# New first loads, fillers ahead of the first products, a fourth buffer for transposed q and k, and a re-planned instruction list

## The chip, the cores and the metric

The kernel runs on one NeuronCore of a Trainium2 chip. The core has five instruction streams that run side by side, each strictly in its own order: TensorE (PE, matrix products), VectorE (DVE), ScalarE (ACT), GpSimd (POOL) and SyncE (SP, which issues DMAs). They wait for one another through semaphores. The metric is the device time of one execution in microseconds; lower is better. Beside the times stands the profile of one execution, whose span runs from the first to the last instruction.

## The reference

Two layers are computed: a linear attention with a feature map of exponentials, and then a layer normalization with a two-matrix feed-forward block and a residual.

```python
batch, n_heads, seq, head_dim = (8, 8, 576, 64);  d_feat = 128

def phi(x):
    proj = np.einsum('bhsd,df->bhsf', x, w_phi)
    proj = proj - np.max(np.abs(proj), axis=-1, keepdims=True)
    return np.concatenate([np.exp(proj), np.exp(-proj)], axis=-1)
q_p, k_p = (phi(q), phi(k))
kv = np.einsum('bhsf,bhsd->bhfd', k_p, v)
z = np.sum(k_p, axis=2)
num = np.einsum('bhsf,bhfd->bhsd', q_p, kv)
den = np.einsum('bhsf,bhf->bhs', q_p, z)[..., None] + 1e-06
x = (num / den)                      # heads side by side: (8, 576, 512)

mu = np.mean(x, axis=-1, keepdims=True)
var = np.mean((x - mu) ** 2, axis=-1, keepdims=True)
xn = (x - mu) / np.sqrt(var + 1e-06) * g_ln
out = x + np.maximum(xn @ w_ch1, 0.0) @ w_ch2      # 512 -> 2048 -> 512
```

Inputs and output are float32.

## The kernel before, in words

**Tiling.** The 8 batches are taken in 4 pairs. A pair has 8 units, each of two (batch, head) combinations, so there are 32 units, numbered n = 0 to 31. A unit's 2 x 576 positions are 8 full tiles of 128 ("main") and one tile with the last 64 of each half ("tails"). When a pair's units are done, its 1152 rows of x are normalized and go through the feed-forward block in 3 rounds of 384 rows: 16 groups of 4 first products (`hT_ps`, L1055) with a relu each (L1063 on DVE or L1065 on ACT), and then, for each of the 3 tiles of 128 rows, 16 second products (`ch_ps`, L1122), a scaling and residual, and a store from SP.

**A unit.** Its k and q are loaded as float32 (L347), brought to bf16 and transposed so that head_dim lies on the partitions. The first 8 units do that on PE with the identity (`a_trans`, L470 and L478) and copy from PSUM. From unit 8 (`QK_DMA`) on, `a_trans_dma` casts q and k into a bf16 buffer `b` (L536 on DVE, L538 on ACT, L540 on POOL) and SP issues a DMA transpose from it into `qkT` (L559). PE multiplies with w_phi (`pm` L622 and L628, `px` L580 and L581 for the tails, `pt` L637 in transposed form); DVE takes the maximum of absolute values (`m`, L686, L584); ACT takes the exponentials (`eb`, `ea`, `em`, `en`); POOL scales v by them (`vv`, L712 to L721); PE forms kv (L778, L783), which is copied (`KV`, L791), and the numerators (`num`, L829, L835); DVE multiplies and adds them (`numc`, L853, L859) and takes the inverse of the denominator (L863); POOL writes x (L869). Of x come the statistics (L982, L996), the centred rows `xc` (L1000) and their transposes `xT`: by PE for pair 0 (L946, L956), by a DMA transpose issued from SP after that (L969). The first weight matrix is scaled by g_ln in place on DVE after pair 0 (L450).

**Buffers.** There are 3 buffers of transposed q and k (`QB`), 2 of the cast ones (`b16_bufs`), 3 of loaded q, k and v. In PSUM there are two large tiles (A), three single banks (B) and one bank N.

**The order of the work.** The program is written first as a list of operations with the keys that they read and write. `Order.run` then plays it: each engine, when free, takes the ready operation of lowest rank; the order in which the operations were started is the order in which the instructions are emitted, and this holds for all five engines. A rank is a "latest start" counted back from the users plus an offset from the table `OFF` by kind of operation and stage (the first 4 units, the next 4, the rest); products of the feed-forward block also have due times (`DUE`, `BLOCK`). Where an operation names several engines, the one that takes it first has it. DMAs are played as an issue on the queue's engine followed by pieces on two modelled resources (hardware and software queues), and the data counts as there `LAND` us later. On the chip nothing of this planner is left but the order: an instruction that waits holds up all behind it on its engine.

**The start.** Ahead of the list a few instructions are emitted by hand: two loads of w_phi on ACT (L248, L249), the identity on POOL (masks.py), POOL's loads of the tails of q (L262), constants and zero fills on DVE, and two casts of w_phi to `wbk` on POOL (L272). In the list, operations without an instruction stand for their times. Until the planned time `WARM` (45 us), PE gets a filler (L1320), a product of a zero tile `wz` into a part of bank N that nobody reads, whenever it has nothing ready. One such product (L1317) opens the kernel.

Of the kernel before, what the change touches and what calls it, by code (L numbers as in the profile page):

```python
# [10 lines left out]
FP32 = mybir.dt.float32  # L11
# [6 lines left out]
def bcast(ap: bass.AP, dim: int, n: int) -> bass.AP:  # L18
# [5 lines left out]
DUE = 30.89  # L24
BLOCK = 115.16
RELU = -983.1
WARM = 45.0
X_DMA, QK_DMA = 1, 8
TILED = 4
LAND, TURN = 1.7, 0.013  # L30
# [3 lines left out]
        "load": 291.2, "trans": 30.0, "trans.copy": 30.0, "mixed": 49.3, "mixed.max": 23.2,  # L34
        "mixed.exp": 41.8, "k": 19.6, "k.max": 21.4, "k.em": -15.4, "k.exp": -46.8, "en": 15.6,
        "vv": -27.5, "q": 30.1, "q.max": 47.4, "q.em": 15.6, "tails": -42.2, "tails.exp": 7.3,
        "kv": -52.7, "kv.copy": 4.2, "num0": 51.4, "num1": -54.2, "num.dve": 32.4, "g1": 0.0,
        "g2": 0.0, "g3": 0.0, "put": -53.0, "ln": 201.7, "w1": -144.2, "w2": 207.3,
    },
    {  # L40
        "load": -11.5, "trans": -36.9, "trans.copy": 204.6, "mixed": 25.2, "mixed.max": -80.9,
        "mixed.exp": 132.7, "k": -79.5, "k.max": 146.3, "k.em": 53.6, "k.exp": -36.9,
# [6 lines left out]
        "load": 22.6, "trans": 17.7, "trans.copy": 96.2, "mixed": -96.6, "mixed.max": -70.2,  # L49
        "mixed.exp": -34.7, "k": -33.5, "k.max": -145.4, "k.em": -34.3, "k.exp": -84.1,  # L50
# [8 lines left out]
class Op:  # L59
    __slots__ = (  # L60
        "engines", "engine", "us", "emit", "rank", "lag", "deps", "users", "acquire", "release",
        "ready", "left", "number", "due",
# [9 lines left out]

class Order:


    def __init__(self, room):
        self.ops, self.wrote, self.read, self.room = [], {}, {}, dict(room)
        self.filler = (None, 0.0, 0.0, None)
# [28 lines left out]
    def run(self):  # L107
# [21 lines left out]
        while events:  # L129
# [10 lines left out]
            for engine, queue in waiting.items():  # L140
# [29 lines left out]
                elif isinstance(us, Op):  # L170
                    us = 1.1 if us.engine == "ACT" else 0.0
# [1186 lines left out]
```

## Time and profile before

| what | value |
|---|---|
| three runs | 382.18, 382.95, 384.82 us; median 382.95 |
| the profiled execution | 381.13 us, of which its span is 379.3 |
| busy, share of the span | PE 95%, ACT 68%, DVE 67%, POOL 54% |
| granted TensorE clock | 1.00 |
| DMA | 53.31 MB in 91133 packets, mean 141 GB/s |
| DMA transposes | 24 of q and k, 9 of x |

The three runs spread over 0.7% of their median. In the profile an engine is busy while an instruction of its own runs; issuing a DMA does not count, and shows under the engine's name with a q (SPq). A wait is put down to whatever released it last. "x24 | 6.5, 272 | 2.1" after an operation means 24 instructions, 6.5 us busy, 272 ns each, and 2.1 us of idle time of that engine just before them. PE's matmuls overlap, and their ends are modelled, so that the distance from start to start says more of its pace than the duration of one. In the table of stretches the columns are the stretch and its length, busy time and number of instructions of PE, its weight loads, DVE, ACT and POOL, the granted clock, and the DMA engines' share and rate.

### The profile page before, as it was taken

What the parts mean: (1) busy time and instruction counts of PE and PEld (TensorE: products, weight loads), DVE (VectorE), ACT (ScalarE), POOL (GpSimd) and SP (SyncE); (2) the same over time, 40 slices, a digit from 0 to 9 for tenths busy, and PEclk for the clock granted to TensorE, in tenths of its full rate; (3) what the DMA queues carried; (4) which work ended last, traced back from release to release, by engine and by line L of the source; (5) the groups of instructions that cost most, each with busy time, mean ns of one, the idle gap of its engine ahead of it and who ended that gap; (6) DMA issues with size and microseconds to landing.
All of it is one profiled execution on the core that took longest, in us unless ns stands there. A gap on an engine that the chain in (4) does not pass through costs nothing.

```text
span 379.3 us, 9487 instructions
## 1 busy us (share of the span) xinstructions
PE 358.9 (95%) x3626; PEld 220.2 (58%) x3626; DVE 254.8 (67%) x557; ACT 257.9 (68%) x574; POOL 204.4 (54%) x350
## 2 busy tenths in 40 slices
PE   4999979988999999999999999999999999999995
PEld 2988856554656555556566555556565555555543
DVE  3698998988999999987787999787749000000001
ACT  3877898968787876896877878786746534444420
POOL 4787878847785768463967835572562101111031
PEclk9999999999999999999999999999999999999999
DMA  8999699999975499956664274430104230101012
GB/s 223 274 223 279 182 225 214 200 276 248 259 203 181 84 229 178 238 108 202 151 167 128 65 158 139 90 61 7 51 13 89 76 88 29 28 30 54 30 55 84
DMA packets 91133, 53.31 MB, mean 141 GB/s; under 512 B 57488, under 2 KB 86544, under 8 KB 91088
## 3 DMA queue, kind: packets, MB, share of 16 engines
q1 hardware_dynamic: 86000, 47.66, 50.5%
q0 software_dynamic: 4384, 4.46, 7.6%
q10 hardware_dynamic: 704, 0.59, 0.6%
q8 instruction: 28, 0.46, 0.5%
q14 instruction: 17, 0.14, 0.1%
HBM read 36.77 MB, written 9.44 MB: 122 GB/s over the span
## 4 chain that ended last, share of the span: by engine, by line
PE 62%; DVE 18%; DMA 8%; issue 5%; POOL 2%; ACT 2%; SPq 1%; DVEq 0%; POOLq 0%; ACTq 0%
PE hT_ps L1055 25%; PE ch_ps L1122 24%; DVE m L686 5%; DMA qkT<-b 5%; DMA qx<-in_k_dram 3%; PE n_bank L783 2%; DVE st L982 2%; PE pm L628 2%; DVE numc L853 2%; DVE numc L859 2%; PE num L829 2%; DMA xT<-xc 1%; DVE hT L1063 1%; PE pt L637 1%; ACT eb L700 1%
## 5 line engine op out<-in xcount | busy, mean ns | idle before, releaser
L1055 PE MATMUL hT_ps<-xT,w 128*128 128x384 bf16 x768 | 152.1, 326 | 1.9 <-DMA xT<-xc 0.8
L1122 PE MATMUL ch_ps<-w,hT 128*128 128x512 bf16 x560 | 150.2, 379 | 0.1
L1055 PEld LDWEIGHTS <-w 128*128 128x128 bf16 x768 | 71.8, 98 | 59.2 <-issue 4.0
L1065 ACT ACTIVATE hT<-hT_ps 128x384 bf16<-128x384 f32 x120 | 59.1, 492 | 56.9 <-PE hT_ps L1055 56.3
L686 DVE TENSOR_REDUCE m<-pm 128x8 f32<-128x1024 f32 x64 | 76.8, 1212 | 13.9 <-PE pm L628 9.7
L869 POOL TENSOR_TENSOR x<-numc,rden 128x384 bf16<-128x384 f32 (+3 forms) x88 | 45.9, 537 | 55.4 <-DVE rden L863 53.6
L1122 PEld LDWEIGHTS <-hT 128*128 128x128 bf16 x560 | 50.8, 98 | 41.4 <-issue 1.6
L700 ACT ACTIVATE eb<-pm 128x1024 bf16<-128x1024 f32 x64 | 65.1, 1038 | 6.3 <-DVE m L686 6.3
L754 ACT ACTIVATE ea<-pt 128x1024 bf16<-128x1024 f32 x64 | 63.6, 1029 | 5.9 <-PE pt L637 5.5
L1141 POOL TENSOR_TENSOR o<-o,x 128x512 f32<-128x512 f32 x20 | 23.1, 1155 | 75.4 <-ACT o L1135 75.4
L1130 DVE SCALAR_TENSOR_TENSOR o<-ch_ps,rstd,x 128x512 f32<-128x512 f32 x15 | 11.1, 741 | 56.7 <-PE ch_ps L1122 56.6
L712 POOL TENSOR_TENSOR vv<-v,em 128x512 bf16<-128x512 f32 x32 | 34.0, 1062 | 20.3 <-issue 15.9
L1063 DVE TENSOR_SCALAR hT<-hT_ps 128x384 bf16<-128x384 f32 x72 | 39.0, 547 | 8.1 <-PE hT_ps L1055 7.7
L712 POOL TENSOR_TENSOR vv<-v,en 128x512 bf16<-128x512 f32 x32 | 34.0, 1062 | 0.0
L829 PEld LDWEIGHTS <-ea 128*128 128x128 bf16 x512 | 23.6, 97 | 9.9 <-issue 3.1
L783 PE MATMUL n_bank<-vv,eb 128*128 128x65 bf16 x512 | 26.9, 194 | 0.0
L540 POOL TENSOR_TENSOR b<-qk,one 128x1024 bf16<-128x1024 f32 x11 | 20.8, 1895 | 10.4 <-DMA qkT<-b 7.2
L783 PEld LDWEIGHTS <-eb 128*128 128x128 bf16 x512 | 22.3, 98 | 3.7 <-issue 0.3
L982 DVE BATCH_NORM_STATS2 st<-x 128x6 f32<-128x512 bf16 (+1 forms) x44 | 24.4, 580 | 0.0
L853 DVE TENSOR_TENSOR numc<-num,em 128x390 f32<-128x390 f32 (+1 forms) x40 | 20.4, 517 | 5.6 <-PE num L829 3.9
L1320 PE MATMUL n_bank<-wz 128*128 128x120 bf16 x333 | 23.0, 221 | 1.2 <-DVE KV L791 0.8
L829 PE MATMUL num<-KV,ea 128*128 128x65 bf16 x416 | 19.7, 193 | 2.0 <-ACT xT L958 0.9
(91 smaller groups left out, 460.3 us busy)
## 6 DMA issues: line engine op xcount, KB each, us to landing
qk<-in_k_dram SPq DMA_DIRECT2D x32, 256.0 KB, 4.3
v<-in_v_dram SPq DMA_DIRECT2D x32, 256.0 KB, 5.6
out_dram<-o SPq DMA_DIRECT2D x31, 256.0 KB, 2.4
qk<-in_q_dram SPq DMA_DIRECT2D x30, 256.0 KB, 5.8
w<-in_moe_w_ch_dram POOLq DMA_DIRECT2D x8, 512.0 KB, 11.1
out_dram<-o SPq DMA_DIRECT2D x10, 128.0 KB, 2.4
qx<-in_k_dram SPq DMA_DIRECT2D x16, 64.0 KB, 4.8
qx<-in_q_dram SPq DMA_DIRECT2D x14, 64.0 KB, 3.5
```

Of the source, the lines that this page charges most:

```text
L686: nc.vector.reduce_max(out=m, in_=ps, axis=AX.X, apply_absolute_value=True)
L700: nc.scalar.activation(eb, ps, AF.Exp, scale=(1.0, -1.0)[t])
L712: nc.gpsimd.tensor_tensor(out=u["vv"][:, t, 0:MX, 0:D], in0=vb[:, hh, :].rearrange("p (c d) -> p c d", d=D), in1=bcast(e[:, 0:MX], 2, D), ...
L754: nc.scalar.activation(u["EA"][:, t, 0:1024], u["pt"], AF.Exp, scale=(1.0, -1.0)[t])
L783: nc.tensor.matmul(ps[:, t, c // 4, :], EB[:, t, c, :], vv[:, t, c, :], start=False, stop=(t == 0 and c == MX - 1), skip_group_check=True,)
L829: nc.tensor.matmul(ps[t][:, i, :], ea(u, t, c), KV[:, t, c // 4, :], start=True, stop=True,)
L869: nc.gpsimd.tensor_tensor(out=dst, in0=st["numc"][ps_, i : i + n, 0:D], in1=bcast(st["rden"][ps_, i : i + n], 2, D), op=ALU.mult,)
L982: nc.vector.bn_stats(out=pr["st"][:, t, half or 0, :], in_=x[:, t, h0 * D : h1 * D])
L1055: nc.tensor.matmul(st["ps"], w1_sb[:, kc, jj * P : (jj + 1) * P], xT_bufs[(pair * NR + r) % XB][:, kc::KC, :], start=(kc == 0), stop=(kc = ...
L1063: nc.vector.tensor_relu(h_sb, st["ps"])
L1065: nc.scalar.activation(h_sb, st["ps"], AF.Relu)
L1122: nc.tensor.matmul(ch[t], hT[r, jj][:, rt * P : (rt + 1) * P], w2_sb[:, jj, :], start=(jj == 0), stop=(jj == JC - 1),)
```

## The change

The first loads are issued in another order and from other queues: w_phi half from SP and half from ACT, k of unit 0, its tails, k and q of unit 1 from SP, q and v of unit 0 from ACT, the tails of v from POOL. The casts of w_phi move from POOL to DVE, and the zero tile, wanted by the fillers, is written first. PE gets 28 fillers ahead of the list. There are 4 buffers of transposed q and k instead of 3, 3 of the cast ones instead of 2, and a cast is called for three units ahead instead of two. The planner's picture changes: loads, transposes and weights have landing times of their own; a transpose holds its queue for the transfers ahead of it (`Turn`); packets of two queues share only while both move; PE is 1.9 times slower until 5.6 us; and from unit 6 on, lags between engines, landings and packets are taken longer (`SLACK`). The offsets, `DUE` and `BLOCK` have other values, so the emitted order differs on all engines.

```diff
-DUE = 30.89
-BLOCK = 115.16
+DUE = -6.82
+BLOCK = 144.95
+COLD, FIRST = 5.6, 28
+SLACK = ((0.2, 0.0, 0.0, 1.0), (0.35, 1.2, 2.0, 1.05))
-X_DMA, QK_DMA = 1, 8
-LAND, TURN = 1.7, 0.013
+X_DMA, QK_DMA, AHEAD = 1, 8, 3
+LAND, LAND_T, LAND_W, TURN, BARRIER = 2.0, 1.1, 2.6, 0.013, 0.4
...
-                    turn = moving[other] + TURN if free.get(other, 0.0) > now else 0.0
-                    us = us.packets * (us.ns + turn)
+                    backlog[engine] -= us.packets * us.ns
+                    both, each = free[other] - now, us.ns + moving[other] + TURN
+                    if both <= 0:
+                        us = us.packets * us.ns
+                    elif both >= us.packets * each:
+                        us = us.packets * each
+                    else:
+                        us = both + (us.packets - both / each) * us.ns
+                elif isinstance(us, Turn):
+                    ahead = backlog["DMA"]
+                    if free["DMA_w"] > now:
+                        ahead *= 3.4
+                    us = max(us.us, max(0.0, free["DMA"] - now) + ahead - 0.5)
...
+                if engine == "PE" and now < COLD:
+                    us *= 1.9
+                if op.load:
+                    backlog[op.load[0]] += op.load[1]
...
-    QB = 3
+    QB = 4
+    NB16 = 3
...
-    nc.scalar.dma_start(out=wphi_f[0:D, :], in_=w_phi)
+    nc.sync.dma_start(out=wphi_f[0:D, :], in_=w_phi)
     nc.scalar.dma_start(out=wphi_f[D : 2 * D, :], in_=w_phi)
...
+    wz = consts.tile([P, P], BF16, name="wz")
+    nc.vector.memset(wz, 0.0)
     wbk = consts.tile([P, 2, F], BF16, name="wbk")
     nc.vector.memset(wbk, 0.0)
-    for i in range(2):
-        rows = slice(i * D, (i + 1) * D)
-        nc.gpsimd.tensor_copy(out=wbk[rows, i, :], in_=wphi_f[rows, :])
...
+    for i in range(2):
+        rows = slice(i * D, (i + 1) * D)
+        nc.vector.tensor_copy(out=wbk[rows, i, :], in_=wphi_f[rows, :])
...
-    b16_bufs = [consts.tile([P, ST], BF16, name=f"b16_{i}") for i in range(2)]
+    b16_bufs = [consts.tile([P, ST], BF16, name=f"b16_{i}") for i in range(NB16)]
...
+        if tiles:
+            packets, ns, lag = tiles * 8 + BARRIER / 0.018, 0.018, LAND_T + sched.slack[2]
+            us = Turn(1.3)
+        elif queue == "POOL":
+            packets, ns, lag = nbytes / row / 16, 0.096 if row == 2048 else 0.194, LAND_W
+        else:
+            packets, ns, lag = nbytes / row / 16, 0.018 if row == 256 else 0.046, LAND
+            lag += sched.slack[1]
+            us = 0.66 if row == 256 else us
+        ns *= sched.slack[3]
...
-    load_main("k", 0, 1, -4.0, "SP")
-    load_main("q", 0, 1, -4.0, "ACT")
-    load_tails("k", 0, -3.0, "SP")
-    load_main("v", 0, 1, -2.8, "SP")
-    load_main("k", 1, 1, -2.6, "SP")
-    load_main("q", 1, 1, -2.6, "ACT")
-    load_tails("v", 0, -2.4, "POOL")
+    load_main("k", 0, 1, -4.0, "SP")
+    load_main("q", 0, 1, -4.0, "ACT")
+    load_tails("k", 0, -3.0, "SP")
+    load_tails("v", 0, -3.0, "POOL")
+    load_main("v", 0, 1, -3.0, "ACT")
+    load_main("k", 1, 1, -2.6, "SP")
+    load_main("q", 1, 1, -2.5, "SP")
...
+        sched.slack = SLACK[n >= H - 2]
...
-            a_trans_dma(units[QK_DMA])
-        if QK_DMA <= n + 2 < NU and n + 2 > QK_DMA:
-            a_trans_dma(units[n + 2])
+            for m in range(QK_DMA, QK_DMA + AHEAD - 1):
+                a_trans_dma(units[m])
+        if QK_DMA + AHEAD - 1 <= n + AHEAD < NU:
+            a_trans_dma(units[n + AHEAD])
...
+    for _ in range(FIRST):
+        fill()
     sched.filler = ("PE", WARM, mm(1, WN), fill)
```

The table `OFF` keeps its keys; nearly all of its values differ, as in its third row `"w1": 244.8` to `22.7` and `"num.dve": -307.4` to `-231.3`.

More of the change, by code (lines that the diff above doesn't have):

```diff
@@ L61 @@
         "engines", "engine", "us", "emit", "rank", "lag", "deps", "users", "acquire", "release",
-        "ready", "left", "number", "due",
+        "ready", "left", "number", "due", "load",
     )
@@ L403, in load_tails @@
             )
[L404 removed]
+            issue(
+                queue, rank, dst, src, [(key + "x" + str(half), j)], 16384 * TG,
+                row=4096 if queue == "POOL" else 256,
+            )
     def loaded(u, key):
```

112 lines of the change are left out of this document (60 added, 52 removed), and 7 rows, old and new, of the table OFF.

## The prediction

> **What bounds the kernel now.** I read the totals first, then four stretches of the span cut where the chain of work changes its character, then that chain, and last the waits inside the stretches that are not full.
>
> ```profile
> span 379.3 us, 9487 instructions
> PE 358.9 (95%) x3626; PEld 220.2 (58%) x3626; DVE 254.8 (67%) x557; ACT 257.9 (68%) x574; POOL 204.4 (54%) x350
> ...
> core 0: us, PE busy (x) PEld busy (x) DVE busy (x) ACT busy (x) POOL busy (x), PEclk, DMA share, GB/s
> 3.35:54.90 51.55, 44.80 (x765) 38.91 (x765) 41.30 (x89) 40.79 (x96) 38.74 (x82) 1.00 1.07 247
> 54.90:153.60 98.70, 92.77 (x1022) 55.16 (x1020) 91.74 (x199) 77.15 (x170) 71.21 (x124) 1.00 0.93 207
> 153.60:362.10 208.50, 208.30 (x1768) 118.83 (x1768) 118.68 (x254) 137.23 (x306) 88.85 (x136) 1.00 0.35 89
> 362.10:379.30 17.20, 13.03 (x77) 7.25 (x74) 0.97 (x2) 2.55 (x4) 3.46 (x3) 1.00 0.23 77
> ```
>
> TensorE (PE) is busy 95% of the span, but that mean joins unlike stages. From 153.6 to 362.1 us it is busy 208.3 of 208.5 us: nothing done to DMAs or buffers shortens this stretch. The last 17.2 us are the second products of the last tiles and their store. What can move lies ahead of 153.6 us.
>
> ```profile
> L1055 PE MATMUL hT_ps<-xT,w 128*128 128x384 bf16 x192 | 37.5, 326 | 1.1 <-DVE numc L859 0.8 <-DVE numc L853 0.3
> L1122 PE MATMUL ch_ps<-w,hT 128*128 128x512 bf16 x141 | 37.6, 379 | 0.0
> ...
> 148.29 5.28 DMA xT<-xc
> 153.60 0.81 PE hT_ps L1055 x4
> ```
>
> These are the dense-layer products inside 54.9 to 153.6 us, and two pieces of the chain. Pair 0 has 3 rounds of 16 x 4 = 192 first products and 9 tiles x 16 = 144 second ones. All 192 and 141 of the 144 are done in this stretch; then PE goes on with the first round of pair 1 as soon as its transposed input lands, at 153.57 us. So PE ran out of dense work just there, and the end is that landing plus about 225.7 us of full PE and tail. What the change is worth is how much earlier attention of pairs 0 and 1 finishes. The engine nearest to its limit there is VectorE (DVE): 91.74 of 98.70 us, idle 6.96. In the first stretch PE's 44.8 busy us are partly fillers (matmuls on zeros, into a bank nobody reads):
>
> ```profile
> L1320 PE MATMUL n_bank<-wz 128*128 128x120 bf16 x333 | 23.0, 221 | 1.2 <-DVE KV L791 0.8 <-ACT KV L793 0.5
> ...
> 5.26 0.29 POOL L272 CAST wbk<-wphi_f 64x128 bf16<-64x128 f32 x1 [1.12 <-DMA wphi_f<-in_w_phi_dram]
> 12.72 0.40 POOL L721 TENSOR_TENSOR vv<-vx,em 128x130 bf16<-128x130 f32 x1 [1.77 <-DMA vx<-in_v_dram]
> ...
> 3.60 0.61 PE L470 MATMUL qkT_ps<-ident,qk 128*128 128x128 bf16 x4
> 5.60 1.01 PE L622 MATMUL pm<-wbk,qkT 128*128 128x256 bf16 x4 [1.40 <-POOL wbk L272]
> 9.44 2.12 PE L1320 MATMUL n_bank<-wz 128*128 128x120 bf16 x20
> 11.50 0.61 PE L470 MATMUL qkT_ps<-ident,qk 128*128 128x128 bf16 x8
> 12.17 0.60 PE L622 MATMUL pm<-wbk,qkT 128*128 128x256 bf16 x4
> 12.61 1.16 PE L1320 MATMUL n_bank<-wz 128*128 128x120 bf16 x19
> ...
> DVE qkT L485 <- PE qxT_ps L478: 2.8, 1, 2.8
> ```
>
> The start loses time in three places: the weights of phi come second on ScalarE's queue and are cast at 5.26 us; the tails of v land late and hold POOL 1.77 us; and unit 1's transposes stand behind 20 fillers of 2.12 / 20 = 0.106 us each, while 19 later ones take 1.16 us, about half. DVE sits idle 2.8 us for it.
>
> **The change, part by part.**
>
> *First loads.* SyncE (SP) now issues one half of w_phi, then k of unit 0, its tails, k and q of unit 1; ScalarE (ACT) issues the other half, q and v of unit 0. POOL no longer casts w_phi (DVE does: two casts, priced with the 0.22 us row for a small cast below). SP's own rows:
>
> ```profile
> 0.74 0.46 SPq L347 DMA_DIRECT2D qk<-in_k_dram  x1
> 1.25 1.62 SPq L347 DMA_DIRECT2D qx<-in_k_dram  x2
> ...
> 3.74 0.37 SPq L347 DMA_DIRECT2D qk<-in_k_dram  x1
> ...
> 5.73 1.24 POOL L347 DMA_DIRECT2D vx<-in_v_dram  x2 [0.17 <-issue]
> ...
> 77.11 0.22 DVE L536 CAST b<-qx 128x128 bf16<-128x128 f32 x1
> ...
> DMA to landing us min/median/max: 2.8/5.8/7.3
> ```
>
> The last line is for the loads of q and k in the first 14 us. Counting on SP: w_phi about 0.5, k 0.5, tails 1.6, so k of unit 1 goes out near 3.4 instead of 3.74 us and q of unit 1 near 3.8; with the median 5.8 us both are there at about 9.6. In the profile unit 1's main transposes start at 11.50. That is 1.9 us earlier, if the list puts them there. Against it, k of unit 0 and its tails go out 0.5 us later. The tails of v, issued at 5.73 us right behind POOL's two casts, need no longer wait for w_phi; 1.8 us earlier is enough to clear the wait of 1.77. Both halves of w_phi go out together, so the products of 5.60 lose their 1.40 us wait, but unit 0's transposes at 3.60 shift by the same 0.5. What DVE gains at the start I take at **-1.9 us**; the ends are +0.5 (only the later tails count) and -2.8 (all of the idle row). It reaches the end only if DVE has no slack behind it:
>
> ```profile
> DVE numc L853 <- PE num L829: 1.0, 2, 0.6
> ...
> DVE KV L791 <- ACT ea L754: 0.3, 1, 0.3
> ```
>
> Those are the first and last of the four waits of DVE from 14 to 55 us, 2.9 us in all, so most of a shift passes through.
>
> *28 fillers.*
>
> ```profile
> 3.19 0.11 DVE L1316 MEMSET wz<- 128x64 uint32 x1
> ```
>
> The zero tile is now written first on DVE, so near 1.0 us (an estimate: SP issues its first load at 0.74, and the tile takes 0.11) rather than 3.19, and 29 matmuls of 0.106 us end near 1.0 + 3.1 = 4.1 us, when k of unit 0 lands. They cover idle time and cost nothing unless k is early; then at most 0.5 us. Their worth is whether the products of 5.60 take 0.60 instead of 1.01 us; part of the 1.9 above, not added. The granted-clock column reads 1.00 from the start and does not show this halving.
>
> The Trainium skill, page "TensorE: Matmul & The Clock Gate", Part 1, says the array runs at half rate until it has been busy for about 3.4 us of a free-running window, whatever the number of matmuls. The trace agrees roughly: products from 5.60 us on, with gaps, still half pace in the group from 9.44, full pace in the one at 12.17. By it 3.1 us of fillers are just short of one window, so the first products of unit 0 could still be cold: 0.4 us less gain than with warm ones, which leaves the sum as it is within its bounds.
>
> *Buffers and lookahead for transposed q and k.* From unit 8 on q and k are cast to bf16 and transposed by DMA. Before there are 2 cast buffers and 3 transposed ones, and a cast is called for two units ahead; after 3, 4 and three ahead.
>
> ```profile
> ACT b L538 <- DMA qkT<-b: 5.4, 5, 2.5
> ...
> POOL b L540 <- DMA qkT<-b: 6.9, 4, 3.5
> ...
> DVE b L536 <- DMA qkT<-b: 1.2, 1, 1.2
> ...
> DVE m L686 <- PE pm L628: 2.7, 5, 0.8
> DVE numc L853 <- PE n_bank L835: 1.1, 1, 1.1
> ...
> 64.91 6.54 SPq L559 DMA_TRANSPOSE qkT<-b  x1
> ...
> 110.44 1.27 SPq L559 DMA_TRANSPOSE qkT<-b  x1
> ...
> DMA to landing us min/median/max: 3.2/3.5/12.1
> ```
>
> The first five rows are waits from 54.9 to 153.6 us, the last is for all 24 transposes of q and k. The casts wait 13.5 us in sum for a buffer still being read by a transpose, on all three engines, with other work queued in order behind them. A third buffer removes that unless transposes come more than three units late. What is late next is DVE itself. Only what reaches DVE counts: its idle time in this stretch, 98.70 - 91.74 = 7.0 us. The gain is between 0 and 7.0; I take half, **-3.5 us**, nearest to its three rows above (2.7 + 1.2 + 1.1 = 5.0), of which the 1.2 goes surely and the others in part. PE has the room for it: it is idle 5.93 us there.
>
> *The list.* The planner now counts a transpose as holding SP for the transfers queued ahead of it (in the trace 6.54 us under load, 1.27 without), cold matmuls 1.9 times slower, loads as landing 2.0 us late or more, and from unit 6 on it adds slack (1.2 us per load, 2.0 per transpose, 5% per packet). With the new offsets every engine's order changes, and which of DVE, ACT and POOL takes a cast or relu. Counts and durations do not change, and nothing in the trace prices an order; its bounds are those of the stretches: I book it within the two terms, and its ends as rivals. In the full stretch it is worth 0.
>
> **Sum.** The profiled execution took 381.13 us, its span 379.3 and 1.8 around it. 381.13 - 1.9 - 3.5 = 375.7 us, a ratio of 0.986. The median of the three runs, 382.95, lies 0.5% above the profiled execution; 0.986 x 382.95 = **377.5 us**.
>
> **Rivals.**
>
> *DVE takes the place of the waits* (chance 0.15). It is busy 93% from 54.9 to 153.6 us; if the rest is dependence and not late DMAs, only the start gains: 381.13 - 1.9 = 379.2, as a median 381.0. For it: the named DMA wait of DVE is only 1.2 us. Against: ACT and POOL lose 12.3 us to the same cause ahead of exponentials and scaled v that feed PE and so DVE.
>
> *The first loads do not come earlier* (0.09), so that part does not do what it says: 381.13 - 3.5 = 377.6, median 379.4. For it: the DMA engines are busy over their full time in the first stretch (share 1.07), and all the bytes stay. Against: unit 1's wait is behind fillers, not loads alone. The Trainium skill, page "DMA: Bandwidth & Descriptors", section "Issuing engines are not separate DMA queues", says that transfers issued from any engine share the same 16 DMA engines, so a new issuer saves only issue time. The trace's share of 1.07 agrees, and so this rival has a chance of its own.
>
> *The list also shifts work off DVE* (0.18). In the middle stretch DVE does relus that ACT, idle 98.70 - 77.15 = 21.6 us, could do:
>
> ```profile
> L1063 DVE TENSOR_SCALAR hT<-hT_ps 128x384 bf16<-128x384 f32 x25 | 13.6, 542 | 0.4 <-PE hT_ps L1055 0.3
> ```
>
> All 7.0 us of idle and 4 of the 25 relus (4 x 0.54 = 2.2 us) make 381.13 - 1.9 - 7.0 - 2.2 = 370.0, median 371.8.
>
> *Slower: transposes pile up on SP* (0.18). Transposes are asked for three units ahead, with two more at unit 7, just when the DMA engines are fullest:
>
> ```profile
> 50.00:60.00 10.00, 7.49 (x81) 4.76 (x80) 9.13 (x19) 9.51 (x24) 8.29 (x20) 1.00 1.31 199
> ```
>
> SP issues in order; behind a held transpose stand the loads of pair 1 and the next transpose. If one transpose lands at the longest 12.1 instead of the median 3.5 us with no other DVE work placed before its products, DVE stands 8.6 us: 381.13 + 8.6 - 1.9 = 387.8, median 389.7. It decides from the point where a unit's products are listed earlier than its landing; below that the fourth buffer hides it. Against it: the planner now prices just this.
>
> **How the numbers follow.** Forecast 0.40, rivals 0.15, 0.09, 0.18 and 0.18. A measurement of this kernel tells about 1% from no change, so faster means below 379.1 and slower above 386.8. Faster: 0.36 of the forecast, 0.18, and 0.03 of the second rival: 0.57. Within 1%: 0.04 + 0.15 + 0.06 = 0.25. Slower: 0.18. The range goes from 369 us, some 3 us below the best rival since both terms may reach their ends, to 388 us, which takes in a pile-up of 7 us; its worst part is left out.
>
> **What would show it.** The page of the changed kernel should show: first products before 5.6 us and taking about 0.6 us, unit 1's transposes near 9.6; no wait of a cast for a transpose above 1 us; the first round of pair 1 starting 4 to 6 us before 153.6, PE full after that with its stretch still some 208 us long. The start is wrong if unit 1 still begins near 11.5, the middle if the casts' waits vanish and DVE's idle time stays 7 us. The whole is wrong if PE is idle in the stretch that is full now, or if a list meant for late landings leaves ready work waiting in order behind work that is not.

## The result, and the profile after

The changed kernel took 391.65 us (median of 13 runs, 385.37 to 396.58) against 382.76 us for the kernel before on the same chip (13 runs, 380.76 to 384.82). The ratio compares the faster executions of both kernels and leaves out the seven of the changed kernel that took 391.65 us and more: **1.0135, interval 1.0091 to 1.0179**, which makes 387.9 us of the 382.76. Forecast were 377.5 us and a ratio of 0.986. The sign is wrong; the median lies above the range of 369 to 388, and the time by the ratio at its upper end.

The profiled execution took 386.87 us. The totals of its page:

```profile
span 384.9 us, 9494 instructions
PE 360.1 (94%) x3613; PEld 224.9 (58%) x3657; DVE 250.9 (65%) x548; ACT 265.9 (69%) x592; POOL 200.7 (52%) x342
```

Next the same three stretches in both traces (length; busy time of PE, its weight loads, DVE, ACT and POOL; granted clock, DMA share, GB/s), the kernel before first:

```profile
10.00:54.90 44.90, 40.44 (x744) 36.41 (x741) 39.65 (x87) 36.87 (x90) 35.92 (x77) 1.00 1.08 241
54.90:100.00 45.10, 41.26 (x468) 25.31 (x466) 40.23 (x90) 36.45 (x80) 34.88 (x67) 1.00 1.14 234
100.00:158.80 58.80, 56.70 (x597) 33.10 (x596) 56.45 (x119) 45.54 (x100) 38.40 (x60) 1.00 0.79 191
```

and the changed kernel, with a row for all that comes after:

```profile
10.00:54.90 44.90, 39.16 (x677) 36.29 (x678) 33.10 (x69) 32.82 (x79) 30.76 (x67) 0.92 1.11 257
54.90:100.00 45.10, 37.69 (x458) 23.55 (x459) 42.14 (x98) 39.13 (x92) 33.68 (x64) 1.00 1.05 223
100.00:158.80 58.80, 56.94 (x574) 33.33 (x582) 52.80 (x114) 47.56 (x107) 37.95 (x56) 1.00 0.69 175
158.80:375.00 216.20, 214.35 (x1823) 123.29 (x1851) 117.46 (x247) 142.40 (x313) 91.95 (x143) 1.00 0.35 86
```

Between 10 and 54.9 us DVE does 6.55 us less work than before, ACT 4.05 and POOL 5.16. From 158.8 us on PE is as good as full (214.35 of 216.2). So nearly all of the time is lost ahead of that: the first `hT_ps` product starts at 60.2 us (before 54.9), the 64th at 83.3 (72.5); half of that delay is won back by the first product of pair 1, at 158.8 (153.6), and PE ends at 381.1 (375.1). Less than 1 us more is lost behind it: from the first product of pair 1 to its end PE takes 222.4 us here, 221.5 in the kernel before. Three things can be seen on the way.

**The start.** The timeline of the changed kernel:

```profile
1.06 2.96 PE L1356 MATMUL n_bank<-wz 128*128 128x120 bf16 x28
...
1.34 0.60 ACTq L378 DMA_DIRECT2D qk<-in_q_dram  x1
1.38 0.82 SPq L378 DMA_DIRECT2D qk<-in_k_dram  x1
...
5.86 0.40 PE L504 MATMUL qkT_ps<-ident,qk 128*128 128x128 bf16 x4 [1.83 <-DMA qk<-in_k_dram]
...
6.93 0.77 PE L656 MATMUL pm<-wbk,qkT 128*128 128x256 bf16 x4 [0.68 <-ACT qkT L521]
...
10.52 1.06 PE L504 MATMUL qkT_ps<-ident,qk 128*128 128x128 bf16 x8
...
10.00:15.00 5.00, 4.95 (x48) 4.37 (x48) 1.48 (x4) 3.70 (x7) 4.39 (x9) 0.59 1.10 343
```

The k of unit 0 goes out 0.64 us later than before (1.38 against 0.74) and is used 2.26 us later (5.86 against 3.60): a load that was alone at the head of its queue now starts beside the others and takes 4.43 us from issue to landing instead of 2.81. The fillers end at 4.0 us and PE stands for 1.83 us. PE has two paces at the start: four transposes take 0.61 us at half pace, as in the kernel before, or 0.40 at full pace, as here at 5.86. The four products at 6.93 (0.77 us) lie between the 0.61 of full pace and the 1.01 of half; from 8.2 us to about 14 everything runs at half pace, and eight transposes that took 0.61 us before take 1.06. The granted clock from 10 to 15 us is 0.59. Unit 1's first maximum comes at 18.2 us (15.0). The 15.0 is an early one, though: in three other traces of the old start it comes at 16.5 to 16.6.

**A stop at 41.8 us.** Casts of units 8 to 10 are listed where their q has not landed; DVE stands 4.21 us and ACT 5.51, with ready work behind them. POOL stands 4.84 us for its writing of `x`; the profile puts that down to a load of v, but `x` also needs the inverse `rden`, which starts at 50.51 us behind DVE's own stop:

```profile
46.02 0.69 DVE L570 CAST b<-qk 128x1024 bf16<-128x1024 f32 x1 [4.21 <-DMA qk<-in_q_dram]
...
49.64 1.04 ACT L572 CAST b<-qk 128x1024 bf16<-128x1024 f32 x1 [5.51 <-DMA qk<-in_q_dram]
...
50.51 0.18 DVE L897 RECIPROCAL rden<-numc 128x6 f32<-128x6 f32 x1
...
50.77 1.96 POOL L903 TENSOR_TENSOR x<-numc,rden 128x192 bf16<-128x192 f32 x6 [4.84 <-DMA v<-in_v_dram]
```

**Transposes beside weight loads.** The chain of work that ended last, from 40 to 90 us, and then the issues of the second weight matrix (POOL) and of SP:

```profile
40.95 5.69 DMA qk<-in_q_dram
...
55.92 11.17 DMA qkT<-b
67.30 0.52 issue
68.10 1.14 DVE m L720
...
78.15 0.60 SPq L593
...
82.27 2.97 DMA qx<-in_k_dram
85.54 2.19 DVE b L570 x3
87.93 2.35 DVE m L720 x2
```

```profile
37.29 0.81 POOL L469 DMA_DIRECT2D w<-in_moe_w_ch_dram  x1
55.95 0.80 POOL L469 DMA_DIRECT2D w<-in_moe_w_ch_dram  x1
59.27 1.55 POOL L469 DMA_DIRECT2D w<-in_moe_w_ch_dram  x2
...
61.31 1.01 SPq L378 DMA_DIRECT2D qk<-in_q_dram  x2
62.42 16.32 SPq L593 DMA_TRANSPOSE qkT<-b  x3
78.84 1.31 SPq L378 DMA_DIRECT2D vx<-in_v_dram  x2
```

One transpose lands 11.17 us after its issue, the next 16.1; three in a row hold SP from 62.4 to 78.8 us, with five loads behind them. Three weight loads of 1 MB each (float32 in memory; the profile counts 512 KB) go out between 55.9 and 60.8 us. In the kernel before they went out at 44.78, 51.65, 62.18 and 63.41, with loads between the transposes of SP. Late landings are not new, though. These are the transposes of q and k issued from 45 to 85 us, five in the kernel before and six in the changed one:

```profile
DMA to landing us min/median/max: 4.2/7.5/12.1
```

```profile
DMA to landing us min/median/max: 3.3/4.6/16.1
```

In sum they take 42.1 and 43.0 us. What differs is which transposes come late, and what the list has put behind them. The waits that the change was to remove are gone, the sum of 13.5 us down to one of 2.2:

```profile
DVE b L570 <- DMA qkT<-b: 2.2, 1, 2.2
```

### The profile page after: what moved, and what is told of

Read it like the earlier page. It is cut to its first block, busy times and chain, and to the rows that moved or that the text cites. A ratio compares the mean times of both kernels' runs of the same rounds, so it can differ in the third digit from the quotient of the medians.

```text
span 384.9 us, 9494 instructions
## 1 busy us (share of the span) xinstructions
PE 360.1 (94%) x3613; PEld 224.9 (58%) x3657; DVE 250.9 (65%) x548; ACT 265.9 (69%) x592; POOL 200.7 (52%) x342
## 3 DMA queue, kind: packets, MB, share of 16 engines
HBM read 36.77 MB, written 9.44 MB: 120 GB/s over the span
## 4 chain that ended last, share of the span: by engine, by line
PE 74%; DVE 10%; DMA 6%; ACT 4%; issue 2%; SPq 2%; DVEq 0%; ACTq 0%
PE hT_ps L1089 28%; PE ch_ps L1156 26%; PE n_bank L1356 3%; PE n_bank L817 3%; DMA qkT<-b 3%; PE pm L662 3%; PE num L863 3%; DVE m L720 2%; DMA qx<-in_k_dram 2%; DVE w L484 2%; PE pt L671 2%; DMA qk<-in_q_dram 1%; SPq L378 1%; DVE st L1016 1%; ACT eb L734 1%
## 5 line engine op out<-in xcount | busy, mean ns | idle before, releaser
L1156 PE MATMUL ch_ps<-w,hT 128*128 128x512 bf16 x519 | 140.3, 379 | 2.3 <-issue 0.6
L1099 ACT ACTIVATE hT<-hT_ps 128x384 bf16<-128x384 f32 x135 | 66.4, 494 | 65.9 <-PE hT_ps L1089 65.5
L903 POOL TENSOR_TENSOR x<-numc,rden 128x192 bf16<-128x192 f32 (+3 forms) x88 | 46.7, 546 | 42.8 <-DVE rden L897 36.8
L734 ACT ACTIVATE eb<-pm 128x1024 bf16<-128x1024 f32 x64 | 64.1, 1029 | 2.4 <-DVE m L720 2.4
L1175 POOL TENSOR_TENSOR o<-o,x 128x512 f32<-128x512 f32 x21 | 24.3, 1158 | 78.8 <-ACT o L1169 78.7
L746 POOL TENSOR_TENSOR vv<-v,em 128x512 bf16<-128x512 f32 x32 | 33.6, 1051 | 46.4 <-issue 42.1
L1164 DVE SCALAR_TENSOR_TENSOR o<-ch_ps,rstd,x 128x512 f32<-128x512 f32 x14 | 10.5, 748 | 53.7 <-PE ch_ps L1156 53.6
L1097 DVE TENSOR_SCALAR hT<-hT_ps 128x384 bf16<-128x384 f32 x57 | 31.3, 551 | 10.7 <-PE hT_ps L1089 9.9
L863 PEld LDWEIGHTS <-ea 128*128 128x128 bf16 x512 | 24.4, 98 | 13.7 <-issue 6.9
L1356 PE MATMUL n_bank<-wz 128*128 128x120 bf16 x364 | 28.8, 233 | 1.7 <-DVE KV L825 1.6
L1356 PEld LDWEIGHTS <-wz 128*128 128x128 bf16 x364 | 24.1, 108 | 3.3 <-issue 2.7
```

The costliest lines, as they stand in the source:

```text
L734: nc.scalar.activation(eb, ps, AF.Exp, scale=(1.0, -1.0)[t])
L746: nc.gpsimd.tensor_tensor(out=u["vv"][:, t, 0:MX, 0:D], in0=vb[:, hh, :].rearrange("p (c d) -> p c d", d=D), in1=bcast(e[:, 0:MX], 2, D), ...
L863: nc.tensor.matmul(ps[t][:, i, :], ea(u, t, c), KV[:, t, c // 4, :], start=True, stop=True,)
L903: nc.gpsimd.tensor_tensor(out=dst, in0=st["numc"][ps_, i : i + n, 0:D], in1=bcast(st["rden"][ps_, i : i + n], 2, D), op=ALU.mult,)
L1097: nc.vector.tensor_relu(h_sb, st["ps"])
L1099: nc.scalar.activation(h_sb, st["ps"], AF.Relu)
```

## The experiments

All ratios are to the kernel before on the same chip, with 95% intervals; a point is 1% of that kernel's time. Where something is listed earlier or later, the list is otherwise kept instruction for instruction.

**The start's cold clock.** 50 fillers instead of 28.

```diff
-COLD, FIRST = 5.6, 28
+COLD, FIRST = 5.6, 50
```

> The changed kernel with 50 fillers instead of 28 ahead of the first products, all else and the emitted order the same; nothing of the computation changes. In the changed kernel PE is at half pace until about 14 us, although 28 fillers ran from 1.0 to 4.0. Theory S (the lost time starts with a cold, late start that every later stage inherits): with PE kept busy until the first load lands at 5.8 us the clock is up by about 6, unit 1's first maximum ends near 15.5 instead of 17.6 us, q of unit 8 lands 2 us earlier than 45.9, and the run is about 2 us faster than the changed kernel (ratio to the kernel before near 1.008). Theory C (the casts of units 8 to 10, placed ahead of their loads, are what costs): the start gains the same 2 us, but DVE still stops for 3 to 4 us near 42 us, and the end moves by less than 1 us. If the clock does not come up, neither moves.

Measured: **1.0157 [1.0071, 1.0244]**. PE runs at full pace (the transposes at 5.66 us, and 79 matmuls from 10 to 15 us against 48):

```profile
5.00:10.00 5.00, 3.59 (x36) 2.42 (x34) 1.82 (x3) 2.30 (x5) 0.15 (x1) 1.00 1.14 266
10.00:15.00 5.00, 4.75 (x79) 4.40 (x78) 2.71 (x6) 5.00 (x11) 4.45 (x9) 1.00 1.11 343
```

Unit 1's first maximum starts at 16.1 us instead of 18.2, and nothing that can be told from noise reaches the end: DVE still stands 4.8 us for q at the later stop.

**The casts behind their loads.** The casts of units 8, 9 and 10 listed some 6 to 10 us later (planned 36.7, 38.1 and 40.1 us before), and unit 8's transpose 2.8 us later (before 39.8).

```diff
...
+CASTS, TURNS = {8: 42.5, 9: 45.0, 10: 50.2}, {8: 42.6}
...
```

> The changed kernel with the casts of units 8, 9 and 10, and the transpose of unit 8, emitted later (planned times 42.5, 45.0, 50.2 and 42.6 us instead of 36.7, 38.0, 39.0 and 39.8); every other instruction keeps its place and nothing is left out. Theory C: the waits of DVE (4.2 us) and ACT (5.5 us) for q of units 8 and 10 go, DVE goes on at 41.8 us, the first hT product comes near 56 instead of 60.2 us, and the run is 4 to 5 us faster than the changed kernel (ratio to the kernel before near 1.00). Theory S: the stop at 42 us covers time that is lost anyway, because what follows waits for the same late loads; the wait moves to another instruction and the end moves by less than 1 us.

Measured: **1.0162 [1.0115, 1.021]**. The stop is gone (DVE 8.38 us busy from 40 to 50 us, 5.76 in the changed kernel), but the first `hT_ps` comes at 62.6 us and no time is won.

**The buffers alone, on the old list.**

```diff
-    qkT_bufs = [consts.tile([P, ST], BF16, name=f"qkT{i}") for i in range(QB)]
-    b16_bufs = [consts.tile([P, ST], BF16, name=f"b16_{i}") for i in range(2)]
+    qkT_bufs = [consts.tile([P, ST], BF16, name=f"qkT{i}") for i in range(QB + 1)]
+    b16_bufs = [consts.tile([P, ST], BF16, name=f"b16_{i}") for i in range(3)]
...
-        u["qkT"] = qkT_bufs[u["n"] % QB]
+        u["qkT"] = qkT_bufs[u["n"] % (QB + 1)]
...
-        b16 = b16_bufs[n % 2]
+        b16 = b16_bufs[n % 3]
...
```

> The kernel before with a fourth buffer of transposed q and k and a third cast buffer, but its emitted order unchanged, so that only waits go. The prediction's middle term: the casts' waits for transposes (13.5 us over three engines from 54.9 to 153.6 us) vanish and the end comes 3.5 us earlier (ratio 0.991). Rival: DVE, busy 93% there, takes their place, and the time stays within 1 us (ratio 0.998 to 1.002).

Measured: **0.9943 [0.9916, 0.9969]**, some 2.2 us. Of the 13.5 us that casts stood for transposes, one wait is left:

```profile
ACT b L538 <- DMA qkT<-b: 0.4, 1, 0.4
```

PE now waits 1.7 us for one transpose instead.

**k first again.** The changed kernel with both halves of w_phi from ACT and k at the head of SP.

```diff
-    nc.sync.dma_start(out=wphi_f[0:D, :], in_=w_phi)
+    nc.scalar.dma_start(out=wphi_f[0:D, :], in_=w_phi)
```

> The changed kernel with both halves of w_phi issued by ACT again, so that k of unit 0 is the first load on SP; emitted order otherwise the same. In the changed kernel k of unit 0 landed at 5.8 us, against 3.5 in the kernel before. Theory S: k lands near 3.6 and the tails of k near 7.2 instead of 8.0 us, unit 0's chain comes about 0.8 us earlier, and the end gains up to 1 us. Theory C: the end moves by less than 0.5 us, since the casts of unit 8 wait for a load that the DMA engines bring at the same time.

Measured: **1.026 [1.0153, 1.0367]**. The products of unit 0 start at 5.83 us (6.93), but the tails of k are late (PE waits 1.94 us for them) and unit 1 stays where it was, at 18.4. Nothing is won by the one load; the interval overlaps that of the changed kernel, so a loss is not shown either.

**The weight loads later.** The last three loads of the second weight matrix listed 56, 59 and 61 us (planned).

```diff
+W2AT = {1: 56.0, 2: 59.0, 3: 61.0}
...
```

> The changed kernel with the last three loads of the second weight matrix issued later by POOL (planned 56, 59 and 61 us instead of 46.5, 50.1 and 50.8); every other instruction keeps its place. In the changed kernel they go out at 56.0, 59.3 and 60.1 us, and the transposes issued at 55.9 and 62.4 land 11.2 and 16.1 us later, against 3.7 for the one before them. Theory W (transposes stand behind weight loads that the list bunches): those two land within 8 us, unit 8's second maximum and unit 9's products come 4 us or more earlier, and the run is 4 us faster than the changed kernel (ratio to the kernel before near 1.003). Theory C (the casts ahead of their loads cost): the stop at 42 us stays and the end moves by less than 1 us.

Measured: **1.0143 [1.0074, 1.0211]**. The two transposes that took 11.2 and 16.1 us land in 6.1 and 5.5; the next two, now beside the weights, take 12.9 and 12.0. The row is that of the transposes from 45 to 85 us:

```profile
DMA to landing us min/median/max: 3.8/6.1/12.9
```

**All three edits together.**

> The changed kernel with 50 fillers, the casts of units 8 to 10 later, and the last three loads of the second weight matrix later, together. If each of the three costs something that the others only hid (the time then comes back at the next late transfer), the three together give 6 us or more against the changed kernel (ratio to the kernel before 0.997 or less), while the first two alone gave nothing. If the list itself is longer for other reasons, the ratio stays above 1.005.

Measured: **1.0135 [1.0062, 1.0209]**. Stretches as above:

```profile
10.00:54.90 44.90, 40.44 (x734) 37.19 (x734) 38.09 (x84) 35.30 (x83) 35.16 (x74) 0.96 1.10 259
54.90:100.00 45.10, 37.72 (x400) 22.69 (x402) 37.26 (x85) 38.85 (x90) 28.44 (x54) 0.90 1.12 208
```

DVE wins back 4.99 us of the 6.55 up to 54.9 us and loses 4.88 in the next 45 (37.26 against 42.14): transposes issued at 69.8 and 74.0 us now take 14.6 and 11.6 us beside the moved weight loads. In this trace PE falls to half pace from about 10.5 to 12.7 us in spite of the 50 fillers, and unit 1's first maximum comes at 17.5 us.

**The start alone, on the old list.** Half of w_phi from SP, its casts on DVE, the zero tile first, 28 fillers.

> The kernel before with the changed kernel's start ahead of the list alone: half of w_phi from SP, its casts on DVE, the zero tile first and 28 fillers; the emitted list is that of the kernel before. The prediction's start term by itself, without the new loads of the list: 1 us or more earlier at unit 1 and 1 us at the end (ratio 0.997). Rival, from the changed kernel's trace: k of unit 0 goes out 0.6 us later and beside four other loads, lands 2 us later, 28 fillers do not bring the clock up, and the end is 1 to 2 us later (ratio 1.003 to 1.005).

Measured: **1.0024 [0.9978, 1.007]**. The trace shows a start that is not better than before, and that fits the missing gain:

```profile
5.00:10.00 5.00, 2.14 (x16) 1.28 (x17) 1.44 (x2) 1.50 (x4) 0.17 (x1) 0.80 1.14 259
10.00:15.00 5.00, 5.00 (x40) 4.21 (x40) 1.34 (x4) 4.48 (x10) 2.81 (x6) 0.51 1.10 342
```

k of unit 0 is used at 6.33 us (3.60 before). The first four transposes take 0.40 us, and from 8.7 to 15 us PE runs at half pace. Unit 1's first maximum comes at 17.1 us.

**Buffers on the old list, weight loads earlier** (planned 38.0, 42.2, 49.0, 58.8).

> The kernel before with a fourth buffer of transposed q and k and a third cast buffer (ratio 0.994 by itself), and the four loads of the second weight matrix issued earlier by POOL (planned 38.0, 42.2, 49.0 and 58.8 us instead of 41.4, 48.3, 58.1 and 59.2), all else in the order of before. Theory W: the transposes of units 9 and 10 land 3 us or more earlier than with the buffers alone (9.3 and 10.9 us from issue), and the ratio is 0.990 or less. Rival: the weights then take the DMA engines from q, k and v of the next units, and the ratio is 0.994 or more.

Measured: **1.0004 [0.9971, 1.0038]**: the buffers' gain is spent. Loads issued from 36 to 60 us, with the time to landing last, first this kernel and then the buffers alone:

```profile
qk<-in_q_dram SPq DMA_DIRECT2D x4, 256.0 KB, 8.4
```

```profile
qk<-in_q_dram SPq DMA_DIRECT2D x4, 256.0 KB, 6.5
```

Transposes of units 9 and 10 land sooner (6.7 and 6.8 us, 9.3 and 10.9 with the buffers alone), q later; unit 6's maxima start at 55.6 us instead of 51.0.

**Start and buffers together, on the old list**: the changed kernel but for its list. To the list belong the order, the choice of engine (DVE has 548 instructions instead of 557, ACT 592 instead of 574, POOL 342 instead of 350) and the new order of the first loads of k, q and v.

> The old list unchanged, with the new start (half of w_phi from SyncE, its casts on VectorE, zero tile first, 28 fillers) and the new buffers (third cast buffer, fourth transposed one) together. Theory: the loss of the changed kernel lies in the re-planned list, so that both hardware parts together on the old list give the product of their own ratios, 1.0024 x 0.9943 = 0.997, between 0.993 and 1.001. Rival: the two parts disturb each other (a later start moves the transposes onto the weight loads), and together they already lose: 1.008 or more.

Measured: **0.9931 [0.9895, 0.9967]**. This is the decisive run: the two parts other than the list together win 0.7%, so **the list costs 1.0135 / 0.9931 = 1.0205**, 2.0% or 7.8 us.

**Buffers and 24 fillers, on the old list and load order.**

> The old list and the old load order with the new buffers; the zero tile is written first and 24 fillers of 0.106 us (2.5 us) stand ahead of the first transposes, which land at 3.55 us. Theory: PE is warm some 2 us sooner, since its first 8 us ran at half pace, and the end gains a part of it over the buffers alone: 0.988 to 0.993, unit 1's first maximum before 14.5 us (15.0 before). Rival: the fillers only fill, PE cools in the gaps behind them, and the ratio is that of the buffers alone, 0.994 plus or minus 0.003.

Measured: **0.9922 [0.9885, 0.996]**, not to be told from the buffers alone. The rival held: the fillers end just as k lands, but the products then wait for `wbk`, and PE is still cold, with 0.61 us for the four transposes as before:

```profile
1.07 2.61 PE L1320 MATMUL n_bank<-wz 128*128 128x120 bf16 x24
3.71 0.61 PE L472 MATMUL qkT_ps<-ident,qk 128*128 128x128 bf16 x4
6.26 1.01 PE L624 MATMUL pm<-wbk,qkT 128*128 128x256 bf16 x4 [1.94 <-POOL wbk L274]
```

**A quarter of the second weight matrix**, in the changed kernel, in the kernel before, and in the old list with start and buffers. The list stays as it is.

```diff
-                out=w2_sb[:, j0 : j0 + JC // NW, :],
...
+                out=w2_sb[:, j0 : j0 + 1, :],
...
-                        w2_sb[:, jj, c0:c1], start=(jj == 0), stop=(jj == JC - 1),
+                        w2_sb[:, jj // 4 * 4, c0:c1], start=(jj == 0), stop=(jj == JC - 1),
...
```

> The changed kernel with its list unchanged, but each load of the second weight matrix brings one of its four blocks of 128 rows, and the products read that block four times: three quarters of these 4 MB are not moved, and the output is not the reference's. To be compared with the same cut of the kernel before, run beside it. Theory A: the new list loses by its weight loads (planned 8 us earlier) colliding with the loads and transposes of units 8 to 11; without them it falls to the other cut kernel within 0.4%, both at 0.985 to 0.995 of the kernel before. Theory B: the list itself is longer on engines that wait for one another; it stays 1.0 to 1.6% above the other cut kernel.

> The kernel before with the same cut of the second weight matrix (one block of four moved, read four times; the output is not the reference's). If the DMA engines bound its first 100 us it gains 1 to 2% (the cut of 3 MB is 13 us at the 234 GB/s of that stretch, partly hidden); if VectorE does, it stays within 0.5%: 0.995 to 1.00. Theory A for the changed kernel expects it within 0.4% of the cut changed kernel, theory B 1.0 to 1.6% below it.

> The old list with the new start, the new buffers and the same cut of the second weight matrix (output not the reference's): what the changed kernel would be but for its list. The cut is worth 0.2% to the kernel before and the two hardware parts 0.7%: 0.991, between 0.987 and 0.995. If the buffers gain only by making room for transposes delayed by the weight loads, the two do not add: 0.994 to 0.998.

Measured: changed kernel **1.0009 [0.9983, 1.0035]**, kernel before **0.9981 [0.995, 1.0011]**, old list with start and buffers **0.9895 [0.9852, 0.9939]**. Without 3 of the 4 MB the changed kernel wins 1.26 points, the kernel before 0.19 (not to be told from zero), the old list with start and buffers 0.36. The first two lie within 0.4% of each other, as theory A has it, though above the 0.985 to 0.995 that it foretold; and its mark was the wrong one: against the kernel that differs by the list alone 1.1 points remain. The 13 us in the expectation for the kernel before count 3 MB; by the bytes that the profile counts for a load, 1.57 MB in all, the same working gives 6.7 us. The transposes of the changed kernel from 45 to 85 us now land in

```profile
DMA to landing us min/median/max: 3.2/3.5/8.2
```

us instead of 3.3/4.6/16.1.

**The remaining 1.1%.** The changed kernel with the cut, with 50 fillers, and with the later casts as well:

> The changed kernel with the cut of the second weight matrix and 50 fillers, nothing else (output not the reference's). With the weight loads in the way 50 fillers gained nothing, though unit 1 began 2.1 us earlier. Theory A: that gain was eaten at the weight loads; with them cut it reaches the end: 0.994 to 0.998 against 1.0009. Theory B: it is eaten by the order itself: 0.999 to 1.003.

> The changed kernel with three causes taken away at once: three quarters of the second weight matrix are not moved (its output is not the reference's), 50 fillers instead of 28, and the casts of units 8, 9 and 10 placed 4 to 11 us later, behind their loads. Theory A: these three are all that the new list loses; it comes down to the old list with the same buffers, start and cut, within 0.4% (0.988 to 0.994 of the kernel before). Theory B: about 0.8% belong to the list itself, to engines waiting for one another; it stays at 0.997 to 1.002, near the 1.0009 with the cut alone.

Measured: **1.0001 [0.9972, 1.0031]** and **1.0007 [0.9981, 1.0033]**. Theory B: neither the cold start nor the casts are in it, as far as the intervals of some 0.3% can tell. With 50 fillers unit 1 starts 2.2 us earlier (16.2, 18.4) and is level again by unit 7 (59.5, 58.6).

**Loads between the transposes.** The five loads behind the three transposes on SP listed between the first and the second: two loads of tails of v, two of v and one of a tail of k, planned at 66.8 to 69.1 us before.

```diff
-GATE = (("k", 3), ("k", 3), ("v", 3), ("v", 3))
+LOADS = {486: 63.30, 488: 63.31, 498: 63.32, 500: 63.33, 869: 63.335}; GATE = (("k", 3), ("k", 3), ("v", 3), ("v", 3))
...
```

> The changed kernel's list with one edit on SyncE: the five loads of the next group (tails of v twice, v twice, one tail of k), which stand behind three transposes in a row and waited from 62.4 to 78.8 us, stand between the first and the second of them. Theory A (the pile on SyncE is what the order itself costs): v and the tails land some 10 us sooner and the ratio falls from 1.0135 to 1.000 to 1.008. Theory B (the transposes' landing behind the weight loads is the limit, and loads brought forward only join them): the second and third transposes land later by what the loads move, about 4 us, and the ratio stays at 1.011 to 1.018.

> The same edit with three quarters of the second weight matrix not moved (output not the reference's), where the three transposes in a row still hold SyncE from 61.2 to 72.5 us. Theory A: the loads behind them were the remaining 1.1% or a good part of it; from 1.0009 the ratio falls to 0.990 to 0.996. Theory B: SyncE waits there for casts that are not ready, the loads behind are early enough, and nothing changes: 0.998 to 1.004.

Measured: **1.0152 [1.0098, 1.0206]** with the whole matrix and **1.0014 [0.9992, 1.0036]** with a quarter. In the latter the five loads go out 7 us earlier and nothing follows from it:

```profile
60.26 3.71 SPq L593 DMA_TRANSPOSE qkT<-b  x1
65.41 1.30 SPq L378 DMA_DIRECT2D vx<-in_v_dram  x2
66.76 1.92 SPq L378 DMA_DIRECT2D v<-in_v_dram  x2
```

In the former a single transpose, issued behind the weight loads, still holds SP:

```profile
67.81 9.74 SPq L593 DMA_TRANSPOSE qkT<-b  x1
77.64 1.31 SPq L378 DMA_DIRECT2D vx<-in_v_dram  x2
```

So the loads that queue behind the transposes are not the price. The weight loads are part of it: taking three quarters of them away is worth 1.26 points to the new list. How they cost it is not shown by itself, since the transposes beside them take no longer in sum than before; the rest lies elsewhere in the order.

## Why the prediction was wrong

**The step that failed is "I book it within the two terms"**, the price of nothing for the new list. It was the largest term of all: +7.8 us (2.0%, with an uncertainty of 0.6 points), the old list with the same start and buffers at 0.9931 against 1.0135. About 0.9 points are its sensitivity to the second weight matrix: 1.26 less the 0.36 that the old list with the same buffers and start wins by the same cut. That difference comes from four intervals and is uncertain by some 0.8 points, so it is barely clear of zero. The other 1.1 points (1.0009 against 0.9895, uncertain by 0.5) stay with a warm start and casts behind their loads, and, in another run, with SP free for loads.

A part of those 1.1 points can be placed. From the first product of pair 1 to PE's end the kernels with the new list take 222.4 us and those with the old list and more buffers 221.3, also where weight loads or other loads are moved: the new list leaves 51 weight loads of PE more for that stretch (1893 against 1842), with their products. That is 1.07 us, 0.3 points. Which part of the order holds the other 3 us or so, ahead of that stretch, **stays open**. The trace of the last kernel has its first product of pair 1 at 154.3 us, where the old list with start and buffers has it at 154.4; but the latter has the whole matrix, and its profiled execution (381.47 us) is 1.5 us above its median, so the two do not show the difference.

**Start, -1.9 us: wrong.** Alone it measures 1.0024, and start with buffers against buffers alone 0.9931 to 0.9943: nothing that can be told from zero. Both runs keep the old order of the first loads of k, q and v, so the new order of these stands in no run by itself. The products of unit 0 start at 6.93 us in the changed kernel (foretold: before 5.6), unit 1's transposes at 10.52 (near 9.6). Two counts failed. "k of unit 0 and its tails go out 0.5 us later" left out that they also land later beside the other first loads: issued 0.64 us later, k lands 4.43 us after its issue instead of 2.81 and is used 2.26 us later. The prediction had named the rule for it, in the Trainium skill, page "DMA: Bandwidth & Descriptors", section "Issuing engines are not separate DMA queues", and given the case 0.09; the trace agrees with it. And the fillers were counted as covering idle time until k lands at 4.1 us. k landed at 5.8, and PE stood 1.8 us.

The other rule weighed there, of the Trainium skill, page "TensorE: Matmul & The Clock Gate", Part 1, says that the array runs at half rate until it has been busy for about 3.4 us of a free-running window. The traces agree with what the prediction made of it, that after 3.1 us of fillers the first products could still be cold, and show both cases: with the same 28 fillers the first four transposes take 0.40 us, full pace, in five traces and 0.61, half pace, in four. In the five PE falls back to half pace afterwards, in the changed kernel from 8.2 to about 14 us; in the four it stays at half pace until 11.8 us or later. With 50 fillers it is at full pace from 5.7 or 7.5 us on in three traces, and falls to half pace for 2 us in the fourth. But the clock did not reach the end: with unit 1's first maximum at 16.1 us instead of 18.2 the ratio is 1.0157 against 1.0135.

**Middle, -3.5 us: right in mechanism, too large.** The waits of casts for transposes vanish as foretold; on the old list this is worth 2.2 us (1.2 to 3.2), where 3.5 were taken. The lookahead of three gave nothing by itself: with two the planner emits the very same list.

**The rival on the slow side** came nearest in size: one transpose at 12.1 us gave 389.7, measured are 11.2 and 16.1 us and 391.65 (387.9 by the ratio). Its place was right too, SP's queue at units 8 to 12. Part of this is luck, for its price was DVE standing 8.6 us for such a transpose. DVE is idle only 2.96 us from 54.9 to 100 us (4.87 before), and the work that it is behind by, 6.55 us, is missing ahead of 54.9 us. Its cause was only half named: the prediction put it down to transposes asked for earlier, and the runs put a part (0.9 points, uncertain by 0.8) down to the weight loads. "The planner now prices just this" was no argument against it: the planner does hold SP 13.1 us for that transpose (planned 50.2 to 63.3 us), and its list has a late transpose there all the same.

**The sign that was foretold came**: "a list meant for late landings leaves ready work waiting in order behind work that is not". The stop at 41.8 us is just this, by casts on DVE and ACT, with POOL waiting behind DVE; but taking it away brought nothing, and in that run the first `hT_ps` product still came late, at 62.6 us. What could have been seen ahead: the list was the one part with no price in any row, it changed every engine's order in a stretch where the DMA share is above 1, and it stood in the sum with nothing.

## What to carry to other kernels

Where a change bundles buffers, a new start and a re-planned order, the order is a term of its own, and in a stretch with a DMA share above 1 its price on the slow side is to be bounded by late landings (here 11 to 16 us, up to 12 in the kernel before, where 3.5 is the median), not set to zero. The most direct test is the one that came late here: the new parts on the old list. A wait that is removed ahead of such a stretch need not be a gain: three stops were removed here singly and together, for none, and in the two runs that moved the weight loads later transposes came late instead. Of the parts on trial the best kernel is the old list with the new start and buffers (0.9931), or with the buffers and 24 fillers (0.9922); the intervals do not tell them, nor the buffers alone (0.9943), apart.

## What the runs showed of the hardware

- In the changed kernel the DMA transposes of q and k issued from 99 us on, when the weight loads have landed, land 3.2 to 4.6 us after their issue; beside loads of 1 MB from POOL's queue they take up to 16.1 us, in the kernel before up to 12.1. With a quarter of those bytes the median from 45 to 85 us falls from 4.6 to 3.5 us and the maximum from 16.1 to 8.2. The weight loads are not the only cause: with the buffers alone one transpose takes 8.7 us at 137.9 us, with no weight load under way.
- The issue of one transpose can hold SP 11.50 us in the changed kernel and 6.54 in the kernel before, and all that SP issues next stands behind it.
- Cutting 3 MB of 4 was worth 0.2% to the kernel before (not to be told from zero) and 1.3% to the changed one, at nearly the same DMA share (1.08 and 1.11 from 10 to 54.9 us, 1.14 and 1.05 from 54.9 to 100): here the share does not tell how much a list suffers by a load. That the time of its issue does is not shown: loads issued earlier took the buffers' gain from the old list (0.9943 to 1.0004), loads issued later gave the new one nothing (1.0143).
- The granted clock read 1.00 in the kernel before while its matmuls ran at half pace (20 fillers in 2.12 us at 9.44 us, 0.106 us each), and 0.59 in the changed one for the same pace. In the kernel before the first record of the clock comes at 11.34 us, and ahead of it the column shows 1.00. There the distance of matmuls tells the pace, the column does not.
